# Two-part broadcast of softmax reciprocals, and a different order of the last heads' value groups, in an attention and FFT kernel

## Chip, cores, metric

One core of one Trainium2 chip. The metric is the device time of one execution in microseconds (us); a profile has its own span, some 1.7 us shorter than the time of the same execution. Profiles name the engines PE (TensorE matmul), PEld (its weight loads), DVE (VectorE), ACT (ScalarE), POOL (GpSimd) and SP (SyncE, which here issues nearly all DMAs; SPq is its queue).

## The reference, cut

Two layers, each an FFT filter (A) followed by an attention with a recurrent memory (B). Only B matters here: 32 heads of 128, 2048 tokens in 64 segments of 32, 8 memory rows.

```python
def _B_ref(x, mem0, Wq, Wk, Wv, Wo, seg_len):          # cut
    for s in range(n_seg):
        h = concatenate([mem, x[:, s*seg_len:(s+1)*seg_len]], axis=1)
        q, k, v = (einsum('btd,dhe->bhte', h, W) for W in (Wq, Wk, Wv))
        scores = where(mask, einsum('bhqe,bhke->bhqk', q, k) * Dh**-0.5, -1e9)
        o = einsum('bhqk,bhke->bhqe', softmax(scores), v)
        o = einsum('bhte,hed->btd', o, Wo)
        mem = o[:, :M]; outs.append(o[:, M:])
# reference(): x += A(layernorm(x)); x += B(layernorm(x)); and both once more
```

## The kernel before

It computes all segments of a head at once. A head's exponentials P are not normalised before the value matmul. The sums of P come from matmuls with ones, ScalarE turns them into reciprocals (Ln, then Exp of minus that), and they are written to DRAM as one row of 4 x 535 floats, which a broadcast DMA spreads to all 128 partitions:

```python
def sums_back(h):                                       # cut
    nc.scalar.activation(out=R, in_=R, func=ACTF.Exp, scale=-1.0)
    nc.sync.dma_start(out=Rd[h]..., in_=R[0:128:32, :])
    if h % 2 or h == H - 2:                             # two heads at a time; head 30 alone
        for a in range(h if h == H - 2 else h - 1, h + 1):
            nc.sync.dma_start(out=Rbs2[a % 2], in_=Rd[a][0:1, :].to_broadcast([128, 4 * NR]))
```

The value matmuls of a head are cut into five groups of queries (four of 15 segments, one of 4). Each group goes to one of two PSUM buffers, and VectorE empties it, multiplied by the broadcast row. Group g uses quarter g of the row; the small group 4 uses a piece of each quarter:

```python
def value_group(h, P, Rb, oT, g_):                      # cut
    pso = pa.tile([128, 512], FP32, name="pso", tag="pso")          # two buffers
    for i, (t, (_, lo, hi, off)) in enumerate(runs[g_]):
        nc.tensor.matmul(pso[...], lhsT=V[...], rhs=P[...], ...)
    if h == H - 1: ...                                  # head 31: the "wide" tile, see below
    elif g_ < NG - 1: r = Rb[:, NR * g_:NR * g_ + NR]
    else: rq = Rb.rearrange("p (s n) -> p s n", n=NR)[...]
    nc.vector.tensor_tensor(out=oT..., in0=byclass(po), in1=rx, op=ALU.mult)
    nc.vector.tensor_tensor(out=oTm..., in0=po[:, :, SEG], in1=rm, op=ALU.mult)
    if g_ == 0: nc.vector.tensor_tensor(out=oTm[:, h, 0:PRE], ...)
```

The order on the engines is written by hand. `merge(dense, dep)` spreads the dependent jobs `dep` (scores, sums, value groups, empty pauses) among the projections `dense`. At step 31 and at step 32, the parts that matter:

```python
else:                                                   # h == H - 1
    dep = [pause, pause]
    for f, p in zip(v0, parts): dep += [f, p]           # v0: value groups of head 28
    ...
elif h == H:                                            # cut; no projections are left
    wide = [... sums_wide(P[h - 1], Rb[h - 1], g_) ...] # head 31: sums with 128 wide ones,
    fill = begin()                                      # its reciprocals need no broadcast
    for n in range(NG):
        if n > 1: groups.pop(0)()                       # value groups of head 30
        wide[n]()
        fill.pop(0)()                                   # 4 matmuls of an output tile
    groups.pop(0)()
    for f in fill: f()
    post[0]()
    tail = begin()
    for f in groups: f(); tail.pop(0)()
else:                                                   # h == H + 1
    merge(tail, values(H - 1))                          # value groups of head 31
```

## Time and profile before

| | |
|---|---|
| time, median of the first 3 runs | 1562.96 us (1561.68 to 1563.09) |
| span of the profile | 1561.0 us |
| TensorE busy, idle | 1532.8 us, 28.2 us |
| broadcasts | 62 of 1070 KB |
| VectorE waiting for broadcasts | 52.8 us in 27 places |

The lines behind this stand in the prediction below. How to read such a profile: TensorE is 98% busy, so only places where it waits can give time back. Per-engine waits tell who ended a wait; the timeline of TensorE marks each wait in brackets; the chain that ended last says where the wait came from. By engine, that chain reads (share of the span):

```profile
PE 91%; DMA 3%; DVE 2%; ACT 2%; issue 1%; POOL 0%; SPq 0%; DVEq 0%; ACTq 0%; POOLq 0%
```

The 3% of DMA are some 47 us of transfers on the chain, but TensorE is idle for only a small part of them. The rest is time in which TensorE had other work, so the chain's share is not what can be won.

### The profile page before, as it was taken

How to read it: one execution, taken by the hardware profiler on the slowest of the kernel's cores; microseconds unless marked ns; L12 is line 12 of the kernel's file. 1: busy time of each engine (PE TensorE's matmuls, PEld its weight loads, DVE VectorE, ACT ScalarE, POOL GpSimd, SP SyncE). 2: the span in 40 equal slices, each digit the busy share in tenths (PEclk: the TensorE clock that was granted, in tenths of full speed). 3: DMA queues.
4: the chain of work that ended last, by engine and by line, in shares of the span. 5: the costliest groups of instructions: out<-in, count | busy, mean ns of one | idle time of the engine just before them, and what ended most of it. 6: DMA issues, size and time to landing. Idle time of an engine off the chain costs nothing.

```text
span 1561.0 us, 36510 instructions
## 1 busy us (share of the span) xinstructions
PE 1532.8 (98%) x14482; PEld 1078.2 (69%) x14483; DVE 807.2 (52%) x2414; ACT 771.6 (49%) x2251; POOL 234.4 (15%) x327
## 2 busy tenths in 40 slices
PE   7999999999999999999999999999999999999998
PEld 6776666666666666677777766666666666666776
DVE  6873545555455555633367545655455545553111
ACT  5584555556555565511136655556555565562000
POOL 3520111112111121100034101112111121110000
PEclk9999999999999999999999999999999999999999
DMA  4681344334433444636114514343433434327242
GB/s 170 219 304 31 110 147 144 137 134 139 158 132 137 150 125 151 190 105 184 51 49 156 185 51 143 137 142 131 167 128 139 151 121 174 124 99 230 68 128 65
DMA packets 159764, 214.86 MB, mean 138 GB/s; under 512 B 7136, under 2 KB 133096, under 8 KB 151648
## 3 DMA queue, kind: packets, MB, share of 16 engines
q1 hardware_dynamic: 159008, 210.14, 40.9%
q8 instruction: 115, 1.88, 0.5%
q0 software_dynamic: 576, 2.30, 0.5%
q14 instruction: 65, 0.53, 0.1%
HBM read 167.32 MB, written 45.10 MB: 136 GB/s over the span
## 4 chain that ended last, share of the span: by engine, by line
PE 91%; DMA 3%; DVE 2%; ACT 2%; issue 1%; POOL 0%; SPq 0%; DVEq 0%; ACTq 0%; POOLq 0%
PE psk L1135 18%; PE psv L1201 18%; PE psx L1480 17%; PE psq L1135 17%; PE pso L1284 4%; PE pss L1211 4%; PE ab L427 2%; DMA bB_S<-Rd 2%; PE psg L585 1%; PE psl L1238 1%; PE psq L1159 1%; PE X L458 1%; PE psu L519 1%; PE psm L911 1%; PE ps L332 1%
## 5 line engine op out<-in xcount | busy, mean ns | idle before, releaser
L1135 PEld LDWEIGHTS <-bB_S 128*128 128x128 bf16 x3180 | 261.4, 97 | 181.1 <-DMA bB_S<-in_B_Wk_dram 1.1
L1194 DVE CAST bB_S<-psk 128x495 bf16<-128x495 f32 (+3 forms) x320 | 191.6, 599 | 276.7 <-PE psk L1135 272.2
L1480 PE MATMUL psx<-Wo_sb,bB_S 128*128 128x320 bf16 x2048 | 288.3, 299 | 0.1
L1214 ACT ACTIVATE bB_S<-pss 128x269 bf16<-128x269 f32 (+5 forms) x576 | 208.9, 386 | 139.8 <-PE pss L1211 139.5
L1480 PEld LDWEIGHTS <-bB_S 128*128 128x128 bf16 x2048 | 196.9, 98 | 74.1 <-DVE bB_S L1298 0.7
L1179 ACT ACTIVATE bB_S<-psq 128x96 bf16<-128x96 f32 x300 | 152.1, 507 | 174.1 <-PE psq L1135 174.1
L1298 DVE TENSOR_TENSOR bB_S<-pso,bB_S 128x480 bf16<-128x480 f32 (+1 forms) x320 | 192.8, 603 | 79.7 <-DMA bB_S<-Rd 52.8
L1254 POOL TENSOR_TENSOR bB_S<-bB_S,bB_S 128x535 f32<-128x535 f32 x90 | 111.6, 1253 | 797.9 <-DVE bB_S L1246 762.9
L1215 DVE TENSOR_TENSOR bB_S<-bB_S,maskf 128x269 bf16<-128x269 bf16 (+5 forms) x576 | 158.9, 289 | 109.1 <-ACT bB_S L1214 109.1
L1203 ACT CAST bB_S<-psv 128x512 bf16<-128x512 f32 (+1 forms) x288 | 162.4, 564 | 80.9 <-PE psv L1201 80.9
L1201 PE MATMUL psv<-bB_S,B1hT_S 128*128 128x256 bf16 x1360 | 168.8, 272 | 0.0
L1201 PE MATMUL psv<-bB_S,B2hT_S 128*128 128x256 bf16 x1360 | 168.8, 272 | 0.0
L1135 PE MATMUL psk<-B2hT_S,bB_S 128*128 128x495 bf16 (+3 forms) x800 | 164.2, 343 | 0.0
L1135 PE MATMUL psk<-B1hT_S,bB_S 128*128 128x495 bf16 (+3 forms) x800 | 164.2, 343 | 0.0
L1135 PE MATMUL psq<-B1hT_S,bB_S 128*128 128x495 bf16 (+5 forms) x780 | 156.1, 336 | 0.6 <-DMA bB_S<-in_B_Wk_dram 0.5
L1135 PE MATMUL psq<-B2hT_S,bB_S 128*128 128x495 bf16 (+5 forms) x780 | 156.1, 336 | 0.5 <-DMA bB_S<-in_B_Wk_dram 0.5
L1201 PEld LDWEIGHTS <-B2hT_S 128*128 128x128 bf16 x1360 | 129.8, 98 | 24.4
L1201 PEld LDWEIGHTS <-B1hT_S 128*128 128x128 bf16 x1360 | 129.8, 98 | 24.4
L1211 PE MATMUL pss<-bB_S 128*128 128x132 bf16 (+8 forms) x1152 | 137.5, 219 | 0.0
L1211 PEld LDWEIGHTS <-bB_S 128*128 128x128 bf16 x1152 | 95.5, 97 | 55.3
L1284 PE MATMUL pso<-bB_S,bB_S 128*128 128x132 bf16 (+8 forms) x1152 | 118.7, 219 | 4.4 <-DVE oTmf L1301 4.3
L1284 PEld LDWEIGHTS <-bB_S 128*128 128x128 bf16 x1152 | 89.3, 98 | 37.6 <-DVE oTmf L1301 6.9
(293 smaller groups left out, 1424.8 us busy)
## 6 DMA issues: line engine op xcount, KB each, us to landing
bB_S<-Rd SPq DMA_DIRECT2D x62, 1070.0 KB
oTx_d<-bB_S SPq DMA_DIRECT2D x60, 512.0 KB
bB_S<-oTx_d SPq DMA_DIRECT2D x46, 512.0 KB
bB_S<-in_B_Wq_dram SPq DMA_DIRECT2D x32, 320.0 KB
bB_S<-in_B_Wk_dram SPq DMA_DIRECT2D x32, 320.0 KB
bB_S<-in_B_Wv_dram SPq DMA_DIRECT2D x32, 320.0 KB
Wo_sb<-in_B_Wo_dram SPq DMA_DIRECT2D x4, 1280.0 KB
B1wv_S<-in_B_Wv_dram SPq DMA_DIRECT2D x10, 512.0 KB
```

Source lines behind the costliest of these rows:

```text
L1135: nc.tensor.matmul(ps, lhsT=w[:, ch, hh * 128:(hh + 1) * 128], rhs=src[:, ch, lo:hi], start=(ch == 0), stop=(ch == 4))
L1179: nc.scalar.mul(out=qv[:, :, 0:SEG], in_=x_view(ps, o, n)[:, :, 1:SW], mul=scale)
L1194: nc.vector.tensor_copy(out=KTs[h % 2][:, lo:hi], in_=ps[:, 0:hi - lo])
L1201: nc.tensor.matmul(ps[:, i * 256:(i + 1) * 256], lhsT=hT[:, ch, st.hcol((t + i) * 128):st.hcol((t + i) * 128) + 128], rhs=w["Wv"][:, ch, : ...
L1203: nc.scalar.copy(out=V[:, t:t + n, :].rearrange("p a b -> p (a b)"), in_=ps[:, 0:n * 256])
L1211: nc.tensor.matmul(ps[:, off - o0:off - o0 + hi - lo], lhsT=KT[:, t * 128:(t + 1) * 128], rhs=QT[:, lo:hi], start=True, stop=True)
L1214: nc.scalar.activation(out=E[:, 0:n], in_=ps[:, 0:n], func=ACTF.Exp)
L1215: nc.vector.tensor_tensor(out=P[:, o0:o0 + n], in0=E[:, 0:n], in1=bs.mask[:, o0:o0 + n], op=ALU.mult)
L1254: nc.gpsimd.tensor_tensor(out=acc, in0=acc, in1=part, op=ALU.add)
L1284: nc.tensor.matmul(pso[:, lo - q0:hi - q0], lhsT=V[:, t, (h % 2) * 128:(h % 2 + 1) * 128], rhs=P[:, off:off + hi - lo], start=(i == 0), st ...
L1298: nc.vector.tensor_tensor(out=oT.rearrange("p (r s j) -> p r s j", r=16, j=2)[:, :, s0:s0 + ns, :], in0=byclass(po), in1=rx, op=ALU.mult)
L1480: self.tc.nc.tensor.matmul(ps[:, 0:320], lhsT=lhs(h, k // 2), rhs=self.g["Wo_sb"][:, h, c0:c0 + 320], start=(h == 0), stop=(h == H - 1))
```

## The change

Intent: the first two groups of a head need only the low half of the reciprocals, so the low half is sent ahead as a transfer of its own; and at the last heads, where little other work is left, the value groups are moved later in TensorE's order. The diff, cut to the changed lines and those next to them:

```diff
-                    nc.sync.dma_start(out=Rbs2[a % 2], in_=Rd[a][0:1, :].to_broadcast([128, 4 * NR]))
+                    for lo in (0, 2 * NR):
+                        nc.sync.dma_start(out=Rbs2[a % 2][:, lo:lo + 2 * NR], in_=Rd[a][0:1, lo:lo + 2 * NR].to_broadcast([128, 2 * NR]))
@@ step 31
-                            dep = [pause, pause]
+                            dep = [pause] * 4
@@ step 32
-                        if n > 1:
+                        if n > 2:
                             groups.pop(0)()
-                        wide[n]()
-                        fill.pop(0)()
-                    groups.pop(0)()
+                        for f in (wide[n], fill.pop(0)):
+                            f()
                     for f in fill:
+                        groups.pop(0)()
                         f()
```

## The prediction

> **What bounds the kernel now.** I read the page's first part first, then TensorE's own waits, then stretches of 20 us over the whole span, then the timeline at the places where TensorE is not full. The first part of the page:
>
> ```profile
> PE 1532.8 (98%) x14482; PEld 1078.2 (69%) x14483; DVE 807.2 (52%) x2414; ACT 771.6 (49%) x2251; POOL 234.4 (15%) x327
> ```
>
> TensorE is the bound: of 1561.0 us it is idle for 28.2 us, so no change of order alone can be worth more than 1.8%. The next question is how much of the 28.2 us lies where the change acts, the attention heads. The stretches (us of the span, then busy us of each engine, clock, DMA share, GB/s) say it; these are the only ones of the heads' part (about 140 to 655 and 900 to 1420) where TensorE falls under 20.00:
>
> ```profile
> 320.00:340.00 20.00, 19.46 (x192) 13.31 (x190) 8.47 (x30) 11.47 (x32) 4.86 (x4) 1.00 0.30 114
> ...
> 620.00:640.00 20.00, 18.95 (x183) 13.17 (x182) 12.22 (x39) 11.54 (x38) 2.45 (x2) 1.00 0.30 113
> 640.00:660.00 20.00, 18.90 (x187) 13.46 (x185) 12.41 (x37) 9.47 (x23) 2.78 (x3) 1.00 0.87 285
> ...
> 1380.00:1400.00 20.00, 19.36 (x179) 13.43 (x178) 8.18 (x27) 12.63 (x39) 3.70 (x4) 1.00 0.37 139
> 1400.00:1420.00 20.00, 18.84 (x200) 13.68 (x198) 12.55 (x37) 13.81 (x41) 4.75 (x5) 1.00 0.62 202
> ```
>
> They lack 0.54, 1.05, 1.10, 0.64 and 1.16 us, 4.5 us in all. The other 24 us lie before 140 us (10 us of it before the first matmul), between the two halves of the program, and in the last few us, where this change does nothing. TensorE's waits name nearly all of the 4.5 us, and VectorE's waits name its origin:
>
> ```profile
> PE pso L1284 <- DVE oTmf L1301: 4.3, 5, 1.1
> ```
> ```profile
> DVE bB_S L1298 <- DMA bB_S<-Rd: 52.8, 27, 3.2
> ```
>
> Line 1284 is the value matmul of one group of queries into a PSUM tile that has two buffers; line 1298 (and 1299, 1301) empties it on VectorE, multiplied by the broadcast reciprocals. The third group of a head needs the first group's buffer, and the first group needs the broadcast. In the timeline of TensorE, then of VectorE, at the last heads of the first layer:
>
> ```profile
> 624.56 0.41 PE L1284 MATMUL pso<-bB_S,bB_S 128*128 128x132 bf16 x4 [1.00 <-DVE oTmf L1301]
> ...
> 646.35 0.41 PE L1284 MATMUL pso<-bB_S,bB_S 128*128 128x132 bf16 x4 [1.02 <-DVE oTmf L1301]
> ```
> ```profile
> 645.48 0.66 DVE L1298 TENSOR_TENSOR bB_S<-pso,bB_S 128x480 bf16<-128x480 f32 x1 [3.18 <-DMA bB_S<-Rd]
> 646.05 0.16 DVE L1299 TENSOR_TENSOR oTmf<-pso,bB_S 128x15 bf16<-128x15 f32 x1
> 646.13 0.16 DVE L1301 TENSOR_TENSOR oTmf<-pso,bB_S 128x7 bf16<-128x7 f32 x1
> ```
>
> The last emptying ends at 646.29, TensorE goes on at 646.35. The chain that ended last has the cause, the transfers (start, length):
>
> ```profile
> 616.29 7.21 DMA bB_S<-Rd
> ...
> 638.62 6.67 DMA bB_S<-Rd
> ```
>
> So the stalls are 1.00 and 1.02 us in layer one, 0.64 and 1.08 us (same view, at 1390.27 and 1412.11) in layer two, and one of 0.54 us at a middle pair of heads (334.64): 4.28 us. VectorE waits 52.8 us for broadcasts in 27 places, but only in these five did TensorE run out of work. The other pairs repeat every 32.20 us with TensorE full.
>
> **What the Trainium skill says.** "Perfetto Trace Analysis", section DMA Optimizations: splitting a DMA lets some of it start sooner when the DMA engines are generally idle. The trace agrees that there is room: the DMA share is 0.30 in 620 to 640. "DMA: Bandwidth & Descriptors", section Queues, rings and completion order: each DMA engine takes descriptors in ring order. So the low half should land well before the high half, and the high half about when the whole does now; no run has shown it yet. The same page, section Anatomy of one DMA, gives about 2 us of fixed cost per transfer, mostly completion. The trace agrees roughly: the 8.4 KB write of the reciprocals is issued at 636.86 and the broadcast that waits for it at 638.62, 1.76 us later. Hence half the bytes do not take half of 7.2 us. "Perfetto Trace Analysis", section Matmuls: groups rotate through PSUM banks so that emptying one overlaps the next; here two buffers give a head's groups just two groups of slack.
>
> **The change part by part.** *Broadcast in two halves.* 62 transfers of 1070 KB become 124 of 535 KB. Groups 0 and 1 need only the low half, groups 2 and 3 the high half, the small group 4 both. In the stretches by half microseconds from 616, data flow from about 617.0 at 150 to 270 GB/s and from 621.5 at 360 to 460. Summed up, 1096 kB have passed at about 621.9 and the first broadcast landed at 623.5, so completion took 1.6 us. 548 kB have passed at 619.8; with the same 1.6 us the low half lands at about 621.4 (estimate), 2.1 us earlier. At 638.62 the same sum gives 548 kB at 643.1, 1096 kB at 644.45, landing 645.29: 0.85 us after. The low half would land at about 643.9, 1.4 us earlier. Cost: 62 more issues of about 0.37 us on the SP queue, 23 us spread over 1561 us. The second head's broadcast waits for its own small write anyway (up to 1.2 us), and the first head's second issue fits into that wait. Compute engines have the same instructions; the order view shows only their order changed, at the last heads.
>
> *Two more pauses at head 31's step.* In the built order the first value group moves behind one dense block. Now the third group would start at 623.56 but for the stall. Then, by the durations in the timeline: keys end at 620.24, queries 1.34 (621.58), group 0 0.25, values 1.09 (622.92), scores and group 1 0.36 (623.28), keys 1.05 and scores 0.12: 624.45. That is 0.89 us later with no work added. Alone it would cut the 1.00 us stall to 0.11, as VectorE's three instructions end at 624.51 today. With the low half at 621.4, VectorE can empty group 0 as soon as it is done, at about 622. Both parts together leave no stall here, nor at 1390.
>
> *Value groups among the widest tile's fill.* Groups 0 and 1 each move one place later, and the four-matmul output pieces (0.54 us) now stand between all groups. From 643.12: wide sum 0.24, piece 0.54, group 0 0.25, wide sum 0.24, piece 0.54 (644.93), group 1 0.24, small wide sum 0.08, piece 0.54: group 2 wants to start at 645.8, where today it wants to at 645.33. VectorE needs 0.81 us for group 0 and 0.06 to release, so the low half must land by about 644.9; the estimate is 643.9. Without the halves 0.5 us of the stall would stay. A small price may come: the small wide sum now starts at 645.16 and needs a buffer that ScalarE frees (line 1276, third group, 644.45 plus 0.66) at 645.11, so perhaps 0.05 us.
>
> Sum: gain 4.28 us at most if all five go, less 0.1 for the wide sum in two layers, less some 0.2 because the 0.54 us stall depends on one execution's slow transfer: about 4.0 us. 1562.96 - 4.0 = 1559.0 us.
>
> **The rivals.** First, *the low half lands hardly earlier*. For: for the first 4 us the transfer moves at half its later rate whatever is behind it, and if that is a cost per row and not per byte, 128 half rows take as long as 128 whole ones. Against: by bytes half is through at 619.8. Then the delay of the groups alone works, removing 0.89 + 0.47 us in layer one and 0.64 + 0.47 in layer two, 2.5 us: 1560.5. Second, *the stall moves*: to the high half (group 2 and then the small group), to the buffers of the wide sums, or to the output stage's loads (the x tiles are issued from 647.64 and first used by VectorE at 655.51, which leaves room for 2 us). Each could return 0.3 to 1 us: 1559.5 to 1561. Third, *the issue queue becomes late*, delaying weights or stores. Against: these are issued 10 us after the broadcasts and weights are fetched a pair ahead; 0.4 us more should be hidden. A slowdown over 1 us seems unlikely.
>
> **Range and chances.** The repeats of before lie 1.4 us apart (1561.68 to 1563.09). All five stalls gone on a good run: 1558; only the reordering works: 1560.5; nothing: 1563. The range is 1557.5 to 1560.9. A change of 2% would be 31 us, more than all of TensorE's idle time, so faster by over 2% is out of reach; slower by 2% would need a new wait of 1 us in each of 30 steps. Hence 0.99 within 2%.
>
> **What would show it.** Right: line 1284's wait for line 1301 falls from 4.3 us to under 0.5; the stretches 320 to 340, 620 to 660 and 1380 to 1420 are at about 20.00 up to the shift; VectorE's wait for the broadcasts falls from 52.8 us to well under 20; span about 1557. Wrong: VectorE still waits 1.5 us or more at group 0 (rival one); new waits at groups 2 to 4, the wide sums or the output pieces (rival two); or busy TensorE time growing past 1532.8.

## The result, and the profile after

| | before | changed |
|---|---|---|
| median of 6 runs | 1561.98 us (1560.64 to 1563.09) | 1558.60 us (1558.29 to 1559.05) |
| span of the profile | 1561.0 us | 1557.3 us |

The ratio is 0.9979, 95% interval 0.9966 to 0.9992, so 3.4 us by the medians: inside 2%, but clear of zero.

The first part of the page and the chain by engine, changed kernel:

```profile
PE 1531.2 (98%) x14482; PEld 1077.5 (69%) x14483; DVE 815.5 (52%) x2414; ACT 771.7 (50%) x2251; POOL 234.4 (15%) x327
...
PE 94%; DVE 2%; ACT 1%; DMA 1%; issue 1%; POOL 1%; SPq 0%; DVEq 0%; POOLq 0%; ACTq 0%
```

The same matmuls in the same busy time; the DMA share of the chain went from 3% to 1%. The stretches of 20 us that lacked TensorE time before (same columns as in the prediction):

```profile
320.00:340.00 20.00, 20.00 (x200) 14.13 (x189) 9.19 (x31) 12.20 (x34) 4.86 (x4) 1.00 0.37 136
...
620.00:640.00 20.00, 19.95 (x197) 14.32 (x196) 13.08 (x44) 12.83 (x40) 2.44 (x2) 1.00 0.38 111
640.00:660.00 20.00, 19.94 (x193) 14.34 (x192) 13.02 (x40) 9.04 (x22) 2.78 (x3) 1.00 0.90 303
...
1380.00:1400.00 20.00, 19.95 (x193) 14.10 (x191) 12.02 (x38) 11.97 (x40) 2.44 (x2) 1.00 0.39 137
1400.00:1420.00 20.00, 19.93 (x200) 14.49 (x198) 11.43 (x33) 11.15 (x33) 2.78 (x3) 1.00 0.76 268
```

Of 4.5 us that were missing, 0.23 us are. VectorE's wait for broadcasts and its two first emptyings at the last heads of layer one (line numbers are one higher here):

```profile
DVE bB_S L1299 <- DMA bB_S<-Rd: 3.1, 2, 2.2
```
```profile
620.92 0.66 DVE L1299 TENSOR_TENSOR bB_S<-pso,bB_S 128x480 bf16<-128x480 f32 x1 [0.91 <-PE pso L1285]
...
642.08 0.66 DVE L1299 TENSOR_TENSOR bB_S<-pso,bB_S 128x480 bf16<-128x480 f32 x1 [2.05 <-PE pso L1285]
```

52.8 us became 3.1 us. Both first groups now wait for TensorE's matmul (pso), no longer for the transfer: the reciprocals are there first. The 3.1 us are two other waits, one of them at head 30 of layer two, of which more below; neither made TensorE wait.

**Where the time is, end to end.** The prediction added up waits to 4.28 us, yet the span is only 3.7 us shorter. To see where, I compare two fixed points of TensorE's work in both profiles: the start of the first group of line 427 (in layer one's FFT) and the end of the last matmul.

| | first L427 | last matmul ends | between | end of span | tail |
|---|---|---|---|---|---|
| before | 26.99 | 1555.11 | 1528.12 | 1561.0 | 5.9 |
| changed | 26.56 | 1549.61 | 1523.05 | 1557.3 | 7.7 |

The start differs by 0.4 us, which is chance (the changed kernel alone has it at 26.56 here and at 27.89 in a second profile, e9 below). Between the points the change gained 5.07 us, more than predicted. Some 0.7 us of that, here and in every gain below, is a stall that this one profile of the kernel before happened to have (see e2 and e3). After the last matmul it lost 1.8 us, where the prediction said that it does nothing. In the tail, VectorE's last addition and the last 160 KB output follow as before, but SP, which closes the program, shows this (groups of SP's instructions by line: count, durations in ns, first and last start). Before, then changed:

```profile
L1765 SPq EVENT_SEMAPHORE  x9: 17/17/17, 1558.7 to 1559.3; - x9
...
L1804 SPq EVENT_SEMAPHORE  x14: 17/28/28, 1559.4 to 1560.9; - x14
```
```profile
L1766 SPq EVENT_SEMAPHORE  x9: 17/17/17, 1553.3 to 1554.0; - x9
...
L1805 SPq EVENT_SEMAPHORE  x14: 17/28/28, 1555.6 to 1557.2; - x14
```

Nine waits behind the last branch (the kernel ends with a branch over a general path, which is not run here), then fourteen that close the program. Before, one set follows the other in 0.1 us; in the changed kernel there are 1.6 us between them, with nothing recorded on SP. No engine computes then. The trace has 841 SP instructions before and 918 in the changed kernel (62 more transfers and 15 more waits); the closing code itself is the same.

### The profile page after: what moved, and what is told of

Read it like the earlier page. It is cut to its first block, busy times and chain, and to the rows that moved or that the text cites. A ratio compares the mean times of both kernels' runs of the same rounds, so it can differ in the third digit from the quotient of the medians.

```text
span 1557.3 us, 36583 instructions
## 1 busy us (share of the span) xinstructions
PE 1531.2 (98%) x14482; PEld 1077.5 (69%) x14483; DVE 815.5 (52%) x2414; ACT 771.7 (50%) x2251; POOL 234.4 (15%) x327
## 4 chain that ended last, share of the span: by engine, by line
PE 94%; DVE 2%; ACT 1%; DMA 1%; issue 1%; POOL 1%; SPq 0%; DVEq 0%; POOLq 0%; ACTq 0%
PE psv L1201 19%; PE psk L1135 18%; PE psx L1481 18%; PE psq L1135 18%; PE pso L1285 4%; PE pss L1211 4%; PE ab L427 2%; PE psg L585 1%; PE psl L1238 1%; PE psq L1159 1%; PE X L458 1%; PE psu L519 1%; PE psm L911 1%; DMA bB_S<-in_B_Wk_dram 1%; PE psg L1642 1%
```

## The experiments

Nine runs (eight new kernels and the changed one again), 5 rounds each, on three chips (e1, e2, e3, e5; e4, e6, e7; e8, e9); each has its own runs of the kernel before. All were correct. "Between" and "tail" are as in the table above, and the gain is in "between" against 1528.12, the one profile of the kernel before.

| run | median (range) | before, same rounds | ratio, 95% | gain between | tail |
|---|---|---|---|---|---|
| e1 halves alone | 1559.35 (1559.06 to 1559.99) | 1562.07 | 0.9984 (0.9970, 0.9998) | 4.86 | 7.4 |
| e2 order alone | 1559.57 (1558.86 to 1559.89) | 1562.07 | 0.9983 (0.9969, 0.9997) | 3.45 | 5.9 |
| e3 halves at last heads | 1557.75 (1556.80 to 1558.58) | 1562.07 | 0.9973 (0.9959, 0.9987) | 5.04 | 6.1 |
| e4 high half first | 1564.08 (1562.47 to 1564.39) | 1561.49 | 1.0013 (0.9999, 1.0026) | 0.07 | 7.6 |
| e5 sixteen issues | 1557.95 (1557.05 to 1558.20) | 1562.07 | 0.9971 (0.9958, 0.9985) | 5.16 | 5.8 |
| e6 four issues | 1559.38 (1559.13 to 1560.30) | 1561.49 | 0.9988 (0.9974, 1.0002) | 5.07 | 7.6 |
| e7 more fill | 1558.26 (1557.51 to 1558.87) | 1561.49 | 0.9979 (0.9965, 0.9992) | 4.28 | 6.1 |
| e8 fill, layer two only | 1556.93 (1556.87 to 1557.82) | 1562.09 | 0.9970 (0.9956, 0.9983) | 5.81 | 5.8 |
| e9 changed, again | 1559.97 (1559.11 to 1560.34) | 1562.09 | 0.9985 (0.9971, 0.9998) | 5.33 | 7.5 |

The changed kernel itself gave 5.07 and, as e9, 5.33 in "between": 0.26 us is the scatter of that figure from one profile to the next. Totals scatter more: the same kernel gained 3.4 us by the medians at first and 2.1 us as e9. Of the totals that were expected, e2, e3, e4 and e8 came within 0.4 us; e1, e5, e6 and e9 were 0.75 to 1.4 us higher, and e7 1.3 us or more. So the places in the profile decide below, more than the totals.

### Which part gives the gain: halves or order

**e1**: the first hunk of the diff alone, order of before.

> Broadcast in halves, order of before kept. Theory H (the early low half is what matters, the new order is spare): with a low half that lands 4.6 us (pair) and 5.1 us (single head) after its issue, as in the changed kernel's trace, VectorE frees the first group's buffer by about 644.6 where the third group wants it at 645.3, so all five stalls on line 1284 go (under 0.2 us each), TensorE time as in the changed kernel, total within 0.5 us of 1558.6. Theory O (the order is what matters): stalls of the last heads stay at about 1 us each, total about 1561. The tail from the last matmul to the end stays at 7.7 us (as many SP instructions as the changed kernel).

No wait for line 1302 is left among TensorE's matmuls, and the gain of 4.86 us is, within scatter, that of the whole change. In layer one VectorE waited for the low half just 0.58 us, until 5.4 us after its issue at 615.44 (the whole took 7.21 us):

```profile
620.85 0.66 DVE L1299 TENSOR_TENSOR bB_S<-pso,bB_S 128x480 bf16<-128x480 f32 x1 [0.58 <-DMA bB_S<-Rd]
```

Theory H held: with the halves, the order is spare. It is not quite worthless. In the changed kernel's layer two the low half of head 30 came late once: issued at 1400.07, VectorE began at 1405.96, ended group 0 at 1406.78, and the third group started at 1407.24. Counted from the same output piece (at 1400.28 here, at 1400.55 in e1), the new order has that start 0.63 us later than the old one has it in e1, so the 0.46 us of slack came from it. No run shows more than that.

**e2**: the other two hunks alone, whole broadcasts.

> New order of the last heads, whole broadcasts. By the prediction's sums the stalls become 0.11 and 0.5 us in layer one, 0 and 0.6 in layer two, and the middle pair's 0.5 us stays: 1.7 us of 4.3 us left. Tail from the last matmul to the end back at 5.9 us (SP instructions as before). Total about 1562 - 2.6 = 1559.4. Theory O: nothing left at the last heads, 1558.4.

The sums of the prediction can be checked place by place. TensorE's marked waits on line 1284, layer one and layer two:

```profile
645.32 0.41 PE L1284 MATMUL pso<-bB_S,bB_S 128*128 128x132 bf16 x4 [0.42 <-DVE oTmf L1301]
```
```profile
1409.88 0.41 PE L1284 MATMUL pso<-bB_S,bB_S 128*128 128x132 bf16 x4 [0.40 <-DVE oTmf L1301]
```

The pauses nearly removed the stalls of head 28 (none is marked, 0.11 was expected), and the moved groups of head 30 left 0.42 and 0.40 us where 0.5 and 0.6 were expected. The middle pair's stall, which was expected to stay, did not occur: these two are the only waits on the line, 0.82 us where 1.7 was expected. VectorE still waited 50.8 us for broadcasts. The order alone gained 3.45 us, so each part alone gives most of the gain and the parts do not add. Its median of 1559.57 us against e1's 1559.35 us is a tie only because its tail is 1.5 us shorter.

**e4**: e1 with the two halves issued in the other order.

```diff
-                    for lo in (0, 2 * NR):
+                    for lo in (2 * NR, 0):
```

> As the run with halves alone (order of before), but the high half of each broadcast is issued first. Same number, size and order of bytes but for that swap. Theory H (the groups gain only because the half that they need first lands first): the low half now lands as late as the whole did (in the changed kernel's trace the second half landed 0.3 us later than the whole of before), so the stalls on line 1284 come back at about 1 us each at the last heads, 4 to 5.5 us in all, and with the long tail of 7.7 us the total is about 1562 + 1.7 = 1563.7. Rival (smaller transfers as such, or less to wait for per transfer, are enough): stalls stay gone, 1559.4.

The stalls are back. First VectorE, then TensorE, at head 28 of layer one:

```profile
623.50 0.66 DVE L1299 TENSOR_TENSOR bB_S<-pso,bB_S 128x480 bf16<-128x480 f32 x1 [3.32 <-DMA bB_S<-Rd]
```
```profile
624.36 0.41 PE L1285 MATMUL pso<-bB_S,bB_S 128*128 128x132 bf16 x4 [1.74 <-DVE oTmf L1302]
```

The four stalls of the last heads are 1.74, 0.96, 0.43 and 1.17 us, and the gain is 0.07 us. Number and size of the transfers are those of e1. So it is not smaller transfers that help, but that the half needed first lands first. With the longer tail this kernel has the highest median of all, 1564.08 us where 1563.7 was expected. That is 2.6 us over its own before, but the interval of the ratio just includes no change, so the four waits are the firmer proof.

### The tail

**e3**: the changed kernel, with halves only for heads 28 to 30 of each layer.

```diff
-                    for lo in (0, 2 * NR):
+                    n = 2 * NR if h >= H - 3 else 4 * NR
+                    for lo in range(0, 4 * NR, n):
```

> The changed kernel with halves only for heads 28, 29 and 30 of each layer; the other pairs get whole broadcasts. Theory T (the changed kernel lost 1.8 us after the last matmul because its 77 extra SP instructions moved the closing code to a place where SP has to wait for its instructions): the tail is 5.9 us again, the last heads have no stall, the middle pair's 0.5 to 0.7 us is back: about 1557.5. Rival (the longer tail comes of something else, by chance or from the order): tail 7.7, about 1559.3.

The tail is 6.1 us, and the gap on SP is gone (848 SP instructions). One part of the expectation missed: the middle pair's stall did not come back. TensorE's waits list none at line 1286, although the middle pairs have whole broadcasts, for which VectorE waits 46.4 us in 25 places; the gain is 5.04 us. It is missing in e2 and e4 too, where the middle pair's low half comes with the whole broadcast (e2) or after the high half (e4). So the 0.54 us stall was most likely chance of the one execution of before that was profiled, and splitting the other 28 heads' broadcasts gave this profile nothing that can be seen. Whether it makes the times steadier (a range of 0.8 us for the changed kernel, 2.4 us before) stays open: e3 has 1.8 us, and e9 1.2 us.

**e5**: the changed kernel with sixteen useless copies.

```diff
+            if nxt is None and h == 5:
+                pads = g["dram"].tile([16, 64], FP32, name="pads")
+                for i in range(16):
+                    nc.sync.dma_start(out=pads[i:i + 1, :], in_=Rd[h][0:1, i * 64:i * 64 + 64])
```

> The changed kernel plus sixteen tiny copies (256 bytes each, DRAM to DRAM) issued by SP in the middle of layer two's heads, where SP is idle; they do nothing useful. Theory T: sixteen more SP instructions move the closing code past that place, the 1.6 us gap between SP's waits at the end goes, tail 5.9 us, total about 1556.9, faster although it has more work. Rival (the tail depends on how much SP or the DMA queues did): tail 7.7 us or more, total 1558.6.

More work, and a shorter tail: it is 5.8 us again. The median is 1557.95 us (1556.9 was expected), with nothing changed at the heads (gain 5.16). By its own ratio against before it is level with e3; the direct comparison with the changed kernel is over different calls, so the profile's tail is the firmer proof.

**e6**: the same with four copies (923 SP instructions, 5 more than the changed kernel).

> As the run with sixteen tiny copies, but four. Theory T (the SP gap at the end sits at a fixed place of SP's code, 9 waits behind the branch in the changed kernel): the gap of 1.6 us stays and moves four or five waits earlier, so that the nine waits of the branch's line start from before it and end after it (first to last about 2.3 us apart in place of 0.7); tail about 7.7, total about 1558.6. Rival (any added issue removes the gap): tail 5.9, total 1557.

The gap stays and moves. The nine waits of the branch's line, e6:

```profile
L1770 SPq EVENT_SEMAPHORE  x9: 17/17/17, 1553.5 to 1555.9; - x9
```

In the changed kernel they took 0.7 us from first to last, here 2.4 us: the gap now lies among them. In the trace's records it follows the ninth wait in the changed kernel, e1, e4 and e9 (all 918 instructions), and the fourth wait in e6. Five more instructions, five waits earlier: counted from the start, it stands behind the 901st of SP's recorded instructions in all five. With 17 more (e5, e7, e8) it has left the closing code, and with 841 or 848 it is not in it. So the gap belongs to a fixed position in SP's instruction stream. What happens there is inferred: between 1553 and 1555 the only traffic is 8 KB in each us, when the outputs are through, and the page lists queues of kind "instruction". One of these, q14, moved five packets of 8 KB in the last 11 us of the changed kernel and four in those of the kernel before. That fits SP waiting for the next block of its own instructions. No run here takes that fetch away, so the mechanism is a guess, not shown.

### A faster version

Three waits of 0.15 to 0.19 us per layer remained at head 31. VectorE takes up a new group there every 0.97 us, and TensorE has 0.78 us of work in that time (the 1.13 us of the expectation below is not the pace that the trace shows). **e7** moves seven more pieces of the output stage there, on top of e5.

```diff
-                    merge(tail, values(H - 1))
+                    merge(tail + begin(), values(H - 1))
```

> The run with sixteen tiny copies, with a fourth output piece (seven more groups of four matmuls, moved up from the output stage, nothing added) among the value groups of the very last head. Three waits of 0.15 to 0.18 us per layer stand there in all runs so far, because VectorE needs 1.13 us for a group and TensorE has 0.79 us of work between groups; with two or three pieces between groups it has 1.3 us or more. Theory: these six waits go, gain 1.0 us, up to 1.9 if each restart of TensorE costs another 0.15 us: total 1556.2 to 1557 where the sixteen copies alone had 1557.95. Rival: the wait moves to the emptying of the extra piece or its PSUM buffer, no gain or a loss of under 1 us.

Half a miss. Those waits went from 1.9 us in e5 (as the weight loads show them, six places) to 0.4 in two. But in layer one a new wait came, which neither theory had named:

```profile
658.59 0.45 PE L394 MATMUL ps<-bB_S,bB_S 128*128 128x128 bf16 x5 [2.16 <-DVE bB_S L130]
```

Line 394 is the next layer's first matmul on token tile 0, after VectorE's layer norm of it. The moved pieces had been the work that covered that norm. The gain fell to 4.28 us. **e8** therefore moves them in layer two only, which no layer follows:

```diff
+                    merge(tail + (begin() if nxt is None else []), values(H - 1))
```

> The run with sixteen tiny copies, with the extra output piece of the run before in layer two only. In layer one that piece put the next layer's first matmul in front of VectorE's normalisation (one new wait of 2.16 us); layer two has no such follower, and there the heads' end came 0.75 us earlier than without the piece. Theory: 0.75 us better than the sixteen copies alone, about 1557.2, and 1.4 us better than the changed kernel in the same rounds. Rival (the gain in layer two is given back in the output stage): same as the sixteen copies alone, 1557.9.

1556.93 us, gain 5.81 us: 0.65 us better than e5 in "between", where 0.75 was expected, and 3.0 us faster than the changed kernel in the same rounds (**e9**, 1559.97 us; the two ranges do not touch), where 1.4 was expected. Of the 3.0 us between the two spans (1555.2 and 1558.2), 1.7 are the tail, 0.5 the heads, and 0.8 a difference at the start (first L427 group at 27.05 and 27.89), which is chance. e8 has the lowest median and the largest gain in "between". By the ratio (0.9970) it cannot be told from e5 (0.9971) or e3 (0.9973), and it still carries sixteen copies that do nothing but shift code.

> The changed kernel unaltered, as a control on the same chip: 1558.6 again, tail of 7.7 us with SP's gap of 1.6 us at the same wait.

The control has the gap at the same wait, 1.7 us, and a tail of 7.5 us. Its median is 1.4 us above the first measurement of the same kernel, where before is level (1562.09 and 1561.98). Its profile shows part of that at the very start: the first L427 group at 27.89 in place of 26.56.

## Why the prediction was right, and where it was not

- **The bound and the five stalls: right.** TensorE's waits on line 1284, traced through VectorE to the broadcasts, were what the change removed, and all are gone in the changed kernel; the four at the last heads by the change, as e4 shows, the fifth most likely by chance.
- **The landing of the low half: right within 0.3 us in layer one, 0.6 us at worst.** "The low half lands at about 621.4", 5.1 us after the issue; e1's VectorE began 5.4 us after it in the pair. The first rival, that half rows take as long as whole ones, would have put it near the whole's 7.2 us, and falls. For a single head the estimate was 5.3 us (643.9); in layer two of the changed kernel VectorE began 5.9 us after the issue, and the new order hid the rest.
- **The order's own share: right.** 0.11 and 0.5 us were to stay without halves; e2 shows none marked and 0.42 (0.40 in layer two).
- **The size of the stalls' sum: too small.** The term "4.28 us at most" is the sum of the marked idle times; the gain was 5.07 us. A marked wait counts only from the modelled end of the matmul before it. Before, then changed, around the third group of head 28 (start, length):

```profile
623.28 0.28 PE L1211 MATMUL pss<-bB_S 128*128 128x148 bf16 x2
624.56 0.41 PE L1284 MATMUL pso<-bB_S,bB_S 128*128 128x132 bf16 x4 [1.00 <-DVE oTmf L1301]
```
```profile
623.22 0.28 PE L1211 MATMUL pss<-bB_S 128*128 128x148 bf16 x2
623.34 0.40 PE L1285 MATMUL pso<-bB_S,bB_S 128*128 128x132 bf16 x4
```

  In a full stream the group starts 0.12 us after the start of the two score matmuls, while they are still shown as running. In the stalled case it starts 1.28 us after. The stall cost 1.16 us and shows as 1.00. The same holds at all five places: set side by side matmul by matmul (14482 in both), the changed kernel gains 0.71, 1.15, 1.21, 0.79 and 1.25 us on the kernel before there, in order of time, 0.15 to 0.19 more than each marked wait, and next to nothing elsewhere. That is the missing 0.8 us. The Trainium skill, "Perfetto Trace Analysis", section Tensor Engine Instruction, says that the end of a matmul in the profile is estimated, not observed; the trace fits that, with the 0.15 to 0.19 us for each stall.
- **The middle pair: most likely chance.** The prediction took "some 0.2" off for it; e2 and e3 show that it need not occur with whole broadcasts at all. With what it really cost, 0.71 us, the change itself gained about 4.4 of the 5.07 us.
- **"The last few us, where this change does nothing": wrong.** The added issues moved SP's closing code across a position that costs 1.3 to 1.8 us (e1, e4, e6 and e9 have it; e2, e3, e5, e7 and e8 do not). The prediction's third rival, a late issue queue, looked at the issues' time, not at their place in the code.
- **The total: right, partly by two errors that cancel.** 5.07 gained, 1.8 lost after the last matmul and 0.4 of luck at the start make the 3.7 us of the spans; the forecast 4.0 us was the sum of the smaller gain and no loss. The forecast of 1559.0 us lies between the two medians of the changed kernel, 1558.60 and 1559.97. Had the closing code not moved, the time would have been near the range's lower end of 1557.5 (e3 and e5: 1557.75 and 1557.95, single runs down to 1556.80).

## What to carry to other kernels

If a consumer takes a transfer in a known order, send what it needs first as its own transfer and first in the queue; e4 shows that the split without the order gains nothing. On a full TensorE, only the few transfers whose lateness outlasts the other work matter (those of heads 28 to 30 of each layer here). After a change to the number of issued instructions, compare the time behind the last matmul too: a gain can be lost there to the mere position of the closing code. And work moved forward to fill a gap leaves a gap where it stood (e7).

## What the Trainium skill lacked or had wrong

- "DMA: Bandwidth & Descriptors", section Rules for kernel authors, says of two transfers to disjoint partition halves "Don't bother — they serialize". For halves by columns whose consumer takes them in turn, this serial order is the gain: 4.86 us of gain with the low half first (e1), 0.07 us with it last (e4).
- "Perfetto Trace Analysis", section Tensor Engine Instruction, says that a matmul's end is estimated, but not what this does to a gap: here each of five gaps on TensorE cost 0.15 to 0.19 us more than the profile's idle time shows.
- No page gives a gap at a fixed position of SP's instruction stream, or its length: here 1.3 to 1.8 us at the end of the program, moved five waits earlier by five more SP instructions and out of the closing code by 17. If it is a wait for instructions, which is not shown, it would belong to "Runtime: NRT & Kernel Launch", section Instruction fetch mechanics.
- No page has the two speeds of a broadcast of one DRAM row to 128 partitions: in half-microsecond stretches 150 to 270 GB/s for the first 4 us, then 360 to 460 GB/s, in the kernel before (two broadcasts in a row, from 617.0). The single one of head 30 shows it too: 86 to 223 GB/s from 639.5 to 643.0, then 347 to 479 until 644.5. The cause is open.
